# One unit of bit patterns in each of eight groups added up on VectorE, in an attention and MLP block on one Trainium2 core

## The chip, the core and the metric

The kernel runs on one core of one Trainium2 chip. The metric is device time in microseconds (us) of one execution; lower is better. A matmul instruction runs on TensorE (PE in the profile; PEld is its weight load), the exponentials of the softmax on ScalarE (ACT), evictions and bit arithmetic on VectorE (DVE) and GpSimd (POOL), and SyncE (SP) issues the transfers.

## The reference

```python
xn = _layernorm(x)                                  # x: 1 x 2048 x 640, bf16
q, k, v = (xn @ wqkv) split into 32 heads of 20
p = softmax(q @ k.T * 20**-0.5)                     # per head, 2048 x 2048
s = (p @ v, heads joined) @ wo
h = gelu(layernorm(xn) @ w1), its four quarters shifted by 1, -1, 2, -2 rows
x1 = xn + h @ w2
g = silu(x1 + gelu(layernorm(x1) @ w3) @ w4)
out = x + s * g
```

## The kernel before

**Groups.** The attention is worked off in 32 groups: eight quads of four heads, times four chunks `qc` of 512 queries. For each group 16 tiles of 128 keys are scored. A score tile of one head is one matmul with 32 rows of contraction in one of four row groups of the array ("row mode", the matmul of L1623); where a tile stands alone in the order it is done as four products over 32 columns each ("column mode", L1640). The method `score_pair` issues both. A switch between row mode and the column mode of all other products costs time, so the order gathers score tiles into bursts.

**Two ways to an exponential.** Most score tiles go to ScalarE, which writes exp of 1024 scores at a time (L1692, 730 times, plus 13 of double width at L1669). The others go to VectorE: `score_both` turns a score into a number whose 16 bits, read as bf16, approximate the exponential (L1714, 512 scores at a time, into the buffer `U`). One such pattern is coarse, so `block_bits` averages four: pattern 0 is `U` itself, patterns 1, 2 and 3 are `U` plus 32, 64 and 96 in the integer domain, each in one of three buffers `SS`. Patterns 1 and 2 of the unit touched here are made by VectorE (L1602, 4096 numbers), pattern 3 by GpSimd (L1600). A unit holds two blocks; a block is one pair of key tiles.

**Products.** The weights of pattern 0 and pattern 1 are the values `VA` unscaled (`EXP_W` is 1.0 for both), those of patterns 2 and 3 are a scaled copy `VP`. For each block and each pattern there is one product task, four matmuls over the four heads that run side by side (L1614), all accumulating in one PSUM bank. So a unit has eight product tasks. Exponentials of ScalarE are multiplied at L1432.

**Other work in the same stream.** TensorE also does all projections and both MLP branches in column mode (L733, 4 matmuls side by side), whose results VectorE evicts. At the end the output projection (`wob` tasks, L733) is multiplied by the gate on VectorE (L1845), and `cmb` adds the input tile, on GpSimd for the first twelve of 16 row tiles (L1911). Its input tile is fetched by SyncE (L1835) into one of two slots `XR`. The first product of a `wob` tile waits until the `cmb` two tiles earlier has read its slot.

**Order.** Which instruction follows which on each engine is written out in one long string, `TABLE`: two characters name a task, and one more each PSUM or SBUF slot that it takes. `follow` reads it, and `plan_sync` sets the semaphores from the tasks' reads and writes. The engines then run freely; each takes its instructions strictly in that order. The durations given to `T(...)` are a planner's costs; on the chip they do nothing. `lock=True` marks work of VectorE and GpSimd that is kept apart: a GpSimd task also waits for the last such VectorE task ahead of it in the string. `AGAIN` names score tiles that are issued once or twice more, into the same bank with the same result; before the change six products are repeated in this way. `ACC` is a dictionary from group to blocks whose patterns 0 and 1 are summed; it is empty before the change.

Of the kernel before, what the change touches and what calls it, by code (L numbers as in the profile page):

```python
# [656 lines left out]
class Gen:  # L657
# [1229 lines left out]
    def finish_qc(self, qc):  # L1887
# [8 lines left out]
        for nl in range(4):  # L1896
# [14 lines left out]
            T("pool" if onp else "dve", 1420 if onp else c_dve(cfg.D, "2x"), lambda e, sl=sl, addend=addend, res=res: e.tensor_tensor(res, SB2[:, sl, :], addend, op=ALU.add),  # L1911
# [234 lines left out]
    r"F+<%+=&'O''P'Q'R'S+.'+/(&E*v'G+9#+#'Z']$+>&'T+:$+X&+0'+W%+;$+8'^'_+Z+,'++('`'a*x+_#+K%+[+`$+J&+-#+?'b+c&F$+H(#7+G'+1*u+V$+b+L)+U%+o&&G&O&*w,+)*y+I$(P+n'+r'''"
    r"H*|,*(+Y#*t*{,,(&P+M+q,.&+u$,-%+x,/&+v#+y+|*z+A'+^(+])*~*},K$+@&,J%+a)'f&'g,#+B$'h'i'j+h('l$+F'k,L'+i''m'n+N,:&+j%+f$&0,;%,>+e#'o+d,=+s(+t''p'q+g$,0,A%,D,9#,"
    r"8$,B&,E+k+w)'r$+m(,<&+l'+p(+O-.'s't,@%,G$,H#,I$,?&&i'u'v'w+P'x#'y,C%'z'{'|'},N$,O#,W(,Z,X),P#+~,M(Q,w&,x%&p,&,),`',R$,_(,[,Q#,F'c#8'[3%+Q05(M$,c,y',b(N,p&,s%"
    r",S)'~,q'+z+{,t$->)-?(,',r&,u(-@$+},T,e,(,~&-2#-#%-1$(#,5',$-5-4,v,%,i-$#,4((%$(&(',]&,6&,1#,2$,^%,f((()(+#(,,3),a((-(.,{#(*-8(,z$-;,7,g-&%-%&(O(R-9),k-<,|%,d"
    r"-H(-K,U#,V$-'&,l,}(/(0-G)-J,Y)-0&-/%-3%-(($,h-M(-L'-N#-O$-R,j,o,n-P#-k%-j&(1$-Q-U(2-6'-l)-E$-7(-F#.`(Y(a-:((3(4-I',m-)(7((5(8(6-A(-B'(9-=-p&-C&-g#.%)-s-h$(:("  # L2150
    r";-_.$((<-i%-X-*.&#-D(Z#-x&-c$(=-w%+R-[-d#-{-z-e$([(](^-u)06-v((_(`-y&-m.1&-q%-~#-}$-W-V-t.((.2'.)).#)-Z(S(.4.*%-a$.5-`#(T(U.+'.8(.;-b'.9).,&.'(V.<(v(W(X.?-n$"
    r"-o#.-(-f-]/8'-r)/9&./(.0).3'(>../:((w((x(y.7#.6$.:%-Y&1(z-T({-^.I&.>+S.B-S.M#.L$(|.J#(@-|&b.H(?(.N)(A(B.A.D.d(.S'.E.T&.U'.c).=.K.g.P%.O$.Q$0I&.f0J.j(.m.V'.k)"
    r".W&0K.X%.n0L0M.h%.i$.l&.b(.@0N.y&.|/k'/n.a).R.Y.G.q#(E.p$.z%.}.F-+/$&.e#(C(D.s(/%'/(.r).t).C.u'/'.Z07(08.~#/#$09.w'/E(/F)/H/&%/I.x&0:0;.{$0<)(-,(}(F/*.o/5#/6"
    r"$/?(.v/@'.[/4/7#0=$0>0?/U&/+/V%/<$/=#0@/A)0A0C#/.0B/>&/W$450D0E0F0G0H/{)/J#/|(--/K$/;/B/1(~()#/N%)$/D'0P0O/C&/S$/R#)%/,/}#/T(/G')&/-/0)'/L(/M)/Y#/Z$/O/)///X/"
    r"P0#&/j(/~'/^%/Q/d)/m/[)0$$/]$(b&(c/g/c(/b&/a'(d(e0Q(f/_%/f/i$/h%0*)0)(/`(g/e'/q0%/l(/30+)/t)//20R#0S0&$0T/z4O(4R0U/w0V0X$0'$(o0Y0Z0[48(0-&0W4E#4F$0,%4G#0.&49"
    r"'/o/v.]0(0]4;/r4<4H#0^4I$4J'4@(4C/s4N'4?)4>%4=&0/4Q/x/p4U#&Z4S'4T(.^4V$/u/y4B4A$4W(4M&4X4Y004]4L%0_$0`0a014P&46$47#4j'4:)4k(0b0c0d4l%4K0e(0f0g4q$4r#5#&0h0i4s"
    r"#5&0j4w'4z5))5((5*'4D4f4x&4v#4u$4y$(p((q4~'5,(5+)(r4{(s(t57#Ef56$50&4^4Z5%5-)5/'51)4`52((u5559%5:(53&4_5.5J#5I$4a4[4c58&4}')=4|(5<545;4b5K'5$)5H5s5T)5?4o$4n#"
    r"4p&)>()?5S(4h'4g&5')@4d)A5B)B4e5L#5U(5b(5a)5M$(h)C4t5>4i)))(5d5X&5W'5e)*._4m5N$5Z$5^5Q()K5[#5P)5Y#)+5R)),5`'5_&5])-5=5v)5c%5u$5w(5E).5z025t#5V5@5x&6L%5y5~'6K"
    r"&5A5m5}(6%6M(6+#6*$6$5O5G5|)6'&6(%5C6,%6))5D5F61'5{(5g6I$6H#6J$5i5h5f60&(i((j(k5j5k5l6/#6.$64636#'5n6_&)D0k6^'68)67((l6&6;6:0l(m6-62#65#6O)66$6N7H6P(6=(n6b')"
    r"E#)R)F)G6>6m&69)6S#6Q&6R$6T$6n%)H)I6G0m$0n0o)J6@6o%03046X(6A0p6Y'6g#6f$6<6U6]6?6W%6V&6[6D6i))L#)M6h(6j(6Z$6`#6k#6c6a$6d)N)O)P6{%)Q6|&6e6B6v#6t)6w$6u(6y6z6l)0"  # L2160
    r"#7#&6x$7<%7=&)1)26~)6q#7%7>'6}(7$6p$)3)47:&79%716r()o7;#)56C76)72$7+73#75(5o77)6F6s6E7()7()8)97?7.)674(7@&):);)<0q)Y)S&)T)h)U)V7P$8~7A#5p7Q%)W)X7T'787L(7I&7K"
    r")7J'7,7B7)7h#7M)7O7N7g$7k(8(%7R(8)&8*&7S'7&7'7-7U7V7b(7c)7`#0s7a$70)a7f7d#7/7e7*7C8>%8?&8@%)Z#8,)7j#7i$)v7m5q8-(7l)[)]7W7v8&%80$8%&:V8/#8'))^)_8;(82)`8.$8<)7"
    r"n7y8='84%86#8183&87#)b#8+8E)898F(85$8A888G))c8K#8d&8e%)d8N)e)f8g(8f&8h)8:8L$)g8O8B%7p8i'8C&)i#)j)k0r8n(8D#8k#8o)8p%8l$)l)m7s)p(8H8m$)q)r)n8S&)}8V8R'8v(8u)8w)"
    r"8j7r8J$8I#8U)s)t)u8r(8Q'8M(8P&0t8s)8q7x7q8Y8T&7o)w&8X7z%7[&7]'8t#7D7^$7{$7|%)x)y)z){)~%En$*#*$*%*&)|7w*'Eo9&&9)9-$9B#5r7E9E9%%Ep8[7u7tEqErEz%909(*(E{E|Eh#EiE"
    r"j*)EkEl8Z9,%EsEm9/9<)9C$3#Et&EuE}Ev9?E~Ew11)123H$3IEx34#3;(3<3=3>3?8]9F3@13F#8c3J3K3L3M35361437387X$7Y%9;(150u$0v0wEy0x8x0y3&&3'3(3)8`399>163*0z3+1%#1&9I1'1("
    r"1)1*9@)7Z&9A(8_8^7~$92%93&9D(7}#8W8a7_3B$3C3D3E3F8#)95'9$$F%96(9##8b94$8$3G8y3-(3.3/0{)0|0}9'&309L97%9T$9S#9*)0~1#31329U)9+(1=#9.#1$1>1?1@9899$9O9:#9e&1A9J?C"
    r"9r(9d%9q)9h911B9g9=%9K9u&9s'9t'9l#9o9k$9G9M17(9V(9n9W):W18199v$9X&1:1;9b&9c':%#:&$9w9R1<:(:)9Z)9[(:^9H1U(:-#:09f#9{&9]%9|'9P1V1W9}(:,$:*):+(1X:.$1Y9Y1C&9^&:/"
    r"1Z9_'9`):_:31D1E9Q9y$9j(9i)9x%1F1G1H9N9m'9a1+#:o8z1,1-:a1.1/109z):#(:$)1b&1c1d:9:A%:@&?M$:>'1e:'&1f9p1I$:`7F:B%:=(9~1J1K1L:X:b?P1g:Z:c:[:K$1M1N:6:?#:L':1:G':"
# [112 lines left out]
```

## Time and profile before

| what | value |
|---|---|
| median of three runs | 781.76 us (780.97 to 783.34) |
| the profiled execution | 782.75 us, of which its span is 780.9 us |
| granted TensorE clock, mean | 0.999 |
| ScalarE busy | 763.0 us, 98% |
| TensorE matmul busy | 770.5 us, 99% |
| VectorE busy | 698.9 us, 89% |
| GpSimd busy | 441.4 us, 57% |

Times in the profile count from the first instruction. A line such as `L1602 DVE TENSOR_SCALAR out<-in x91 | 110.4, 1225 | 2.0 <-PE` is one group of instructions: source line, engine, operation, shapes, how many; their busy time in us, the mean of one in ns; the idle time of the engine just before them and what ended it. Records of neighbouring instructions on one engine overlap a little, so that the pitch from start to start is shorter than a record.

### The profile page before, as it was taken

What the parts mean: (1) busy time and instruction counts of PE and PEld (TensorE: products, weight loads), DVE (VectorE), ACT (ScalarE), POOL (GpSimd) and SP (SyncE); (2) the same over time, 40 slices, a digit from 0 to 9 for tenths busy, and PEclk for the clock granted to TensorE, in tenths of its full rate; (3) what the DMA queues carried; (4) which work ended last, traced back from release to release, by engine and by line L of the source; (5) the groups of instructions that cost most, each with busy time, mean ns of one, the idle gap of its engine ahead of it and who ended that gap; (6) DMA issues with size and microseconds to landing.
All of it is one profiled execution on the core that took longest, in us unless ns stands there. A gap on an engine that the chain in (4) does not pass through costs nothing.

```text
span 780.9 us, 27979 instructions
## 1 busy us (share of the span) xinstructions
PE 770.5 (99%) x12470; PEld 291.4 (37%) x12470; DVE 698.9 (89%) x1170; ACT 763.0 (98%) x803; POOL 441.4 (57%) x238
## 2 busy tenths in 40 slices
PE   8999999999999999999999999999999999999997
PEld 4433332334434333233434333333334333333454
DVE  8889899988999999988988889998989889897786
ACT  7999999999999999999999999999999999999986
POOL 5676646544566656466564664766454456645733
PEclk9999999999999999999999999999999999999999
DMA  5232532450122333432242331334421123014443
GB/s 174 41 109 59 128 90 58 120 121 24 29 45 54 76 81 76 102 64 45 54 92 55 82 71 33 67 69 69 122 55 29 30 45 87 16 23 136 116 125 104
DMA packets 141352, 58.12 MB, mean 74 GB/s; under 512 B 113728, under 2 KB 136432, under 8 KB 141232
## 3 DMA queue, kind: packets, MB, share of 16 engines
q1 hardware_dynamic: 141232, 56.33, 31.0%
q8 instruction: 98, 1.61, 0.8%
q14 instruction: 22, 0.18, 0.1%
HBM read 34.70 MB, written 10.33 MB: 58 GB/s over the span
## 4 chain that ended last, share of the span: by engine, by line
PE 57%; ACT 40%; DVE 1%; DMA 1%; issue 0%; POOL 0%; SPq 0%
ACT arena L1692 35%; PE psum L733 21%; PE psum L1623 16%; PE psum L1614 10%; PE psum L1432 7%; PE psum L1640 1%; ACT arena L2095 1%; ACT arena L1669 1%; ACT arena L2003 1%; DMA arena<-in_A_x_dram 1%; ACT arena L2123 1%; PE psum L1489 1%; PE psum L1463 1%; PE psum L1493 0%; ACT L1692 0%; PE psum L1079 0%
## 5 line engine op out<-in xcount | busy, mean ns | idle before, releaser
L1692 ACT ACTIVATE arena<-psum 128x1024 bf16<-128x1024 f32 x730 | 676.7, 1106 | 6.6 <-PE psum L1623 4.0
L1600 POOL TENSOR_TENSOR arena<-arena 128x2048 int32<-128x2048 int32 x92 | 330.2, 3598 | 195.9 <-DVE arena L1602 106.3
L1714 DVE TENSOR_SCALAR arena<-psum 128x512 uint16<-128x512 f32 x528 | 341.6, 682 | 36.2 <-PE psum L1623 28.4
L733 PE MATMUL psum<-arena 128*32 128x320 bf16 (+1 forms) x5808 | 331.6, 333 | 0.8 <-POOL arena L1911 0.7
L1623 PE MATMUL psum<-arena 32*128 32x512 bf16 x1908 | 254.3, 384 | 1.6 <-ACT arena L1692 0.6
L1614 PE MATMUL psum<-arena 128*22 128x512 bf16 x2112 | 183.5, 382 | 0.0
L733 PEld LDWEIGHTS psum<-arena 128*32 128x32 bf16 x5808 | 135.6, 96 | 121.1 <-issue 48.6
L1623 PEld LDWEIGHTS psum<-arena 32*128 32x128 bf16 x1908 | 68.2, 91 | 223.4 <-ACT arena L1692 113.3
L1432 PE MATMUL psum<-arena 128*22 128x512 bf16 x1456 | 137.9, 382 | 0.0
L1602 DVE TENSOR_SCALAR arena<-arena 128x4096 uint16<-128x4096 uint16 (+1 forms) x121 | 130.3, 1091 | 2.6 <-PE psum L1614 1.2
L1614 PEld LDWEIGHTS psum<-arena 128*22 128x22 bf16 x2112 | 46.5, 90 | 64.2 <-issue 46.0
L1746 POOL TENSOR_TENSOR arena<-arena 128x512 bf16<-128x512 f32 x30 | 41.7, 1390 | 46.5 <-DVE arena L1602 35.6
L1432 PEld LDWEIGHTS psum<-arena 128*22 128x22 bf16 x1456 | 34.9, 90 | 44.7 <-issue 33.4
L2088 DVE CAST arena<-psum 128x512 bf16<-128x512 f32 x48 | 32.6, 681 | 2.8 <-PE psum L733 2.8
L1299 DVE CAST arena<-psum 128x512 bf16<-128x512 f32 x40 | 27.1, 682 | 6.2 <-PE psum L733 6.0
L1640 PE MATMUL psum<-arena 128*32 128x512 bf16 x328 | 32.1, 381 | 0.0
L1911 POOL TENSOR_TENSOR arena<-arena 128x640 bf16<-128x640 bf16 x12 | 16.8, 1399 | 22.5 <-DVE arena L1539 9.2
L944 DVE BATCH_NORM_STATS2 arena<-arena 128x6 f32<-128x320 bf16 x54 | 24.3, 476 | 2.0 <-DMA arena<-in_A_x_dram 2.0
L1669 ACT ACTIVATE arena<-psum 128x2048 bf16<-128x2048 f32 x13 | 25.6, 1969 | 0.1
L1845 DVE SCALAR_TENSOR_TENSOR arena<-psum,arena 128x320 bf16<-128x320 f32 x32 | 15.2, 482 | 9.1 <-PE psum L733 9.0
L1733 DVE STREAM_TRANSPOSE arena<-psum 128x512 f32<-128x512 f32 x30 | 21.3, 710 | 2.1 <-PE psum L1623 0.9
L2117 DVE TENSOR_TENSOR arena<-psum,arena 128x320 bf16<-128x320 f32 x32 | 15.6, 486 | 6.8 <-PE psum L733 6.6
(135 smaller groups left out, 339.6 us busy)
## 6 DMA issues: line engine op xcount, KB each, us to landing
arena<-in_B_w_dram SPq DMA_DIRECT2D x48, 160.0 KB, 2.7
arena<-arena SPq DMA_DIRECT2D x124, 32.0 KB, 1.9
arena<-in_B_w_dram SPq DMA_DIRECT2D x4, 960.0 KB, 5.5
arena<-in_A_x_dram SPq DMA_DIRECT2D x8, 320.0 KB, 6.0
arena<-in_A_x_dram SPq DMA_DIRECT2D x16, 160.0 KB, 2.4
out_dram<-arena SPq DMA_DIRECT2D x16, 160.0 KB, 2.2
heads<-arena SPq DMA_DIRECT2D x120, 20.0 KB, 2.0
arena<-queries SPq DMA_DIRECT2D x28, 80.0 KB
```

What stands on the lines that cost most here:

```text
L733: ins = e.matmul(pb[32 * c:32 * c + 32, 0:N], lhsT(k, c), rhs(k, c), start=(k == 0), stop=(stop and k == nk - 1), tile_position=(0, 32 * c))
L1432: ins = e.matmul(pb[32 * i:32 * i + 22, 0:512], VA[:, ql, kts[i // 2], i, :], PT[:, slots[i // 2][0].slot, slots[i // 2][0].at(i % 2):slot ...
L1600: return e.tensor_tensor(dst.bitcast(I32), U[:, ub, 0:w].bitcast(I32), bass.AP(c.tensor, c.offset, [list(c.ap[0]), [0, w // 2]]), op=ALU.add)
L1602: fa if onp else lambda e, v=v, dst=dst: e.tensor_scalar(dst, U[:, ub, 0:w], EXP_B[v], None, op0=ALU.add),
L1614: ins = e.matmul(pb[32 * i:32 * i + 22, 0:512], wv, dst[:, at:at + 512].bitcast(BF16), start=first, stop=final, tile_position=(0, 32 * i))
L1623: return e.matmul(out, self.KT[32 * i:32 * i + 32, b, 128 * kt:128 * kt + 128], q, start=True, stop=True, tile_position=(32 * i, 0))
L1640: ins = e.matmul(out[32 * c:32 * c + 32, :], self.KT[:, b, 128 * kt + 32 * c:128 * kt + 32 * c + 32], self.QM[:, gb, i, :], start=True, st ...
L1669: lambda e: e.activation(self.PT[:, hp[0].slot:hp[0].slot + 2, :], self.psum[:, 512 * h0.slot:512 * h0.slot + 2048].rearrange("p (a b) -> ...
L1692: lambda e: e.activation(self.PT[:, hp.slot, :].rearrange("p (a b) -> p a b", b=512), self.banks(hs), AF.Exp, scale=cfg.scale),
L1714: T("dve", c_dve(512), lambda e, h=h, y=y: e.tensor_scalar(U[:, ub, y:y + 512], self.bank(h.slot)[:, :], a_exp, EXP_BIAS, op0=ALU.mult, op ...
L1746: return e.tensor_tensor(OnT.rearrange("p (k d a) -> p a k d", k=4, a=4), Ob[:, :].rearrange("p (a k d) -> p a k d", a=4, k=4), in1, op=AL ...
L2088: T("dve", c_dve(512), lambda e, h=h, fc=fc, i=i, G=G: e.tensor_copy(G[:, i, fc, :], self.wbank(h)[:, 0:512]), reads=[wa], writes=at, name ...
```

## The change

For eight groups (one in each quad) the unit with blocks 2 and 3 gets two new VectorE instructions, each 2048 numbers wide: they add `U` (pattern 0) to the buffer of pattern 1, both read as bf16, in place. The product tasks of pattern 0 of that unit are gone; the products of pattern 1 now take the sum. That is 16 adds more and 16 product tasks (64 matmuls of L1614) fewer in the whole kernel. The code for such a sum was there before, as a transfer issued by GpSimd, but with `ACC` empty it never ran. `AGAIN` becomes empty, so the six repeated score products go. The planner's cost of `cmb` on GpSimd goes from 1420 to 2000. And the string with the order is another one from its 385th entry of 6,939 on, which lies in the first group of the first quad; from there the two orders differ in detail. No other instruction is added or removed.

```diff
--- before.py
+++ after.py
@@ -582,7 +582,7 @@
         self.W7 = (0, 1)
         self.LAST = [[[4, 2]], [[3, 2]]]
         self.HP = True
-        self.AGAIN = {(3, 1, 10, 2): 1, (7, 1, 2, 1): 1, (7, 1, 6, 2): 1, (7, 1, 12, 1): 2, (7, 1, 15, 0): 1}
+        self.AGAIN = {}
         self.EARLY = 4
         self.ND = ([2, 4, 4, 4],) + tuple([5, 4, 5, 4] for _ in range(5)) + ([5, 5, 5, 5], [5, 5, 4, 4])
         self.PP |= {(quad, qc, 0, 2) for quad in range(8) for qc in range(4)}
@@ -594,6 +594,7 @@
         self.NR[6][1] = (107,)
         self.NR[6][3] = ()
         self.NR[7][1] = (107,)
+        self.ACC = {(0, 1): (2, 3), (1, 1): (2, 3), (2, 1): (2, 3), (3, 0): (2, 3), (4, 1): (2, 3), (5, 0): (2, 3), (6, 2): (2, 3), (7, 0): (2, 3)}
         self.ND = ([2, 4, 4, 4], [5, 4, 4, 4], [5, 4, 4, 4], [5, 4, 4, 4], [5, 4, 5, 4], [5, 4, 5, 4], [5, 4, 5, 4], [5, 4, 4, 4])
 
 
@@ -1601,9 +1602,10 @@
                 T("pool" if onp else "dve", 90 + 0.925 * w if onp else c_dve(w, "4x"),
                   fa if onp else lambda e, v=v, dst=dst: e.tensor_scalar(dst, U[:, ub, 0:w], EXP_B[v], None, op0=ALU.add),
                   reads=halves + ([A("CI", v)] if onp else []), writes=dsta, name=f"s{quad}_{qc}_{blocks[0][0]}_{v}", lock=True, due=self.at(self.nact, f"s{quad}"))
-            if acc and v == 1:
-                T("pool", 1000, lambda e, dst=dst: e.dma_start(dst.bitcast(BF16), U[:, ub, 0:w].bitcast(BF16), accum_op=ALU.add, max_dma_last_dim=4096),
-                  reads=halves + dsta, writes=dsta, is_dma=True, nbytes=2 * 256 * w, name=f"acc{quad}_{qc}_{blocks[0][0]}", stream="acc", lock=True)
+            for x in range(len(blocks) if acc and v == 1 else 0):
+                y = slice(2048 * x, 2048 * x + 2048)
+                T("dve", c_dve(2048, "2x"), lambda e, dst=dst, y=y: e.tensor_tensor(dst[:, y].bitcast(BF16), dst[:, y].bitcast(BF16), U[:, ub, y].bitcast(BF16), op=ALU.add),
+                  reads=halves + dsta, writes=dsta, name=f"acc{quad}_{qc}_{blocks[0][0]}" + "y" * x, lock=True, due=self.at(self.nact, f"s{quad}"))
             for n, (j, kts, units) in enumerate([] if acc and v == 0 else blocks):
                 def fn(e, v=v, dst=dst, n=n, j=j, kts=kts, units=units):
                     pb = self.bank(self.PVB)
@@ -1908,7 +1910,7 @@
                     self.wo_mult("wob", n, hh, range(cfg.KC + (qc not in cfg.W7)), SB2[:, sl, :], A("SB2", sl, hh))
             res, resa = (addend, adda) if split else (OS[:, sl, :], [A("OS", sl)])
             onp = n in cfg.PC
-            T("pool" if onp else "dve", 1420 if onp else c_dve(cfg.D, "2x"), lambda e, sl=sl, addend=addend, res=res: e.tensor_tensor(res, SB2[:, sl, :], addend, op=ALU.add),
+            T("pool" if onp else "dve", 2000 if onp else c_dve(cfg.D, "2x"), lambda e, sl=sl, addend=addend, res=res: e.tensor_tensor(res, SB2[:, sl, :], addend, op=ALU.add),
               reads=adda + [A("SB2", sl, 0), A("SB2", sl, 1)], writes=resa, name=f"cmb{n}", lock=True, cls=-2 if split and nl > 1 else 0)
             T("sp", C_SP, lambda e, res=res, n=n: e.dma_start(outv[:, n, :], res),
               reads=resa, writes=[("out", n)], is_dma=True, nbytes=128 * cfg.D * 2, name=f"st_out{n}", stream=f"out{sl}" if n < self.cfg.NT - 1 else "out2",
@@ -2141,109 +2143,109 @@
...
-    r"&2)&J&K(G(J&L*7*0&,'@&3&%*_&*`%*a$*J$*K#*H(&M*I)*L'*M&?#&@&A*N(L#4'A3$&B&C&4(&D*Q&+'$(K&5+(#*E*P(*T*O)&=(*F'/)&N+)&&>'0'1*S#&q#*W#*X$'2'3*Y(&r&s*R%*[(*Z)&t&u"
...
+    r"&2)&J&K(G(J&L*7*0&,'@&3&%*_&*`%*a$*J$*K#*H(&M*I)''*M&?#&@*L'&A&B&C*N&4(&D&5+'#*Q&+($*P(*O)+)#'/#'0*E*T&=('1'2&q)*F*X#*S&*W$&>#4'3&r*Y)&s*Z('4*[)*R%&t*U*V&u+3"
...
```

More of the change, by code (lines that the diff above doesn't have):

```diff
@@ L2147 @@
[L2147 to L2166, printed above, removed]
@@ new lines @@
+    r"$&v+2#*c%*]%*h'*b&+4'*i('I$'J'K'L'M+$#+%$(L*k*d&*l+&('.'N(K*^*G*p'&/&i*n(*s*m)*q)*o&'5('6'7'8'9*r+5$'A+T':&E+6#&N+7%+**e'U$*g&+D'+C(*v*f%*j#'V'W'X'B''Y'C'D'E"
+    r"'Z'F+E('O&+=%+<&+>$'P*y'Q'R&p'S'G'T'H3$*|+.)+/(+0&+#+:$+X%+[+W&+9#+8']#'^'_++(+;)+,)+Z'`'a'b+_%+b+K#+J$+`&+c+?*t&F#+-%+G(+L'+H)&G+1+I)&O(+U$+o&+V#+Y#*w&P*u+n"
+    r"'+r,*(+q,+)*{*x+v%,,$+y+u&,.$,-#*z,/%+M'f#+^)+]('g+x+|'h+@#+A$,K%+a),J&'i'['j*~'e+B&+h(,L'+i)'k(Q*}+F+j&'l&'m'n,;$,:%+e'+f&'o'p+N,>+g('q,=,0+t(+s)+w$+d,8$,9#"
+    r"+l',B&,<#,E+k,A%+m('r$'s't'u,G#,D+O+P,H$+p),?%,@&,I%'v'w,C&'x#'y'z'{'|,O$,N#'},X(,W),[,P(,Z,),w&,x%,F,_',`(#7,#,c,y)3%,&,Q#,R$+}+z,q)-.'~,b,S&,t%'c,p(,r#,',M"
@@ new lines @@
+    r"&Z,s$,u%+~(#+{,~#-?'-2&-5->((M$-#$-@'+Q(N,T,$(O,%,1',z(,2&,(05,v-$&,4%,5$,3$(%&(&,6((',^',]&,a#(((),d,{)(Y(+((,,|%,i,e,7,V&,U'(-,k(*,f-%#-9(-&$-<,Y$-8)(.(/-'"
+    r"(,h,o-0&-/'-;-H(,j-(-M#-L$(0-G),}#8-K-J-3#-1%-4-P&-O(-j&-k',g-N)-R(7&(8(9-l%-F%-6',l-E&-7(-:)(:,m-Q($(1$(2,n(3-I$-A'-B(-U-h$(4(5-g%-)-_-C((6-=-i$(;-X(<-*-p&."
+    r"`(P.%'.$((Z$([-d$-c#-x%-W(=-[-s.&)-D-u'-{-w&-v(-e&(](^(_&0-z-}#(`.2%-~$-V-y(-Y-m-q'.5.((.)).1&.#'-T-`$-a%-t.4.*$.'(S&(T.8(.9).+'.;-b%.,&(R+R(v06+S(E(U(V-n$-o"
+    r"%.<-f(W.-#.0&./'-r)(X/8(/9)-S-Z/:'(@.?.=.6$.7#.3&-|.>(w(-](x.B.:%(y.I&.J((z({..-^(>(?&(A.L$(|.M%.H.D(B.d'.T).c&&b.S(.P#.g.N#.K.U%.@.O$0I(0J.k'.f.W(.V).n.Q$.j"
```

176 lines of the change are left out of this document (94 added, 82 removed).

## The prediction

> **What bounds the kernel now.** I read the page first, then the busy times by stretch, then the groups by shape, and last the waits and the places where ScalarE stands.
>
> ```profile
> span 780.9 us, 27979 instructions
> PE 770.5 (99%) x12470; PEld 291.4 (37%) x12470; DVE 698.9 (89%) x1170; ACT 763.0 (98%) x803; POOL 441.4 (57%) x238
> PE 57%; ACT 40%; DVE 1%; DMA 1%; issue 0%; POOL 0%; SPq 0%
> ```
>
> Busy times by stretch (PE, PEld, DVE, ACT, POOL, then clock, DMA share, GB/s):
>
> ```profile
> 20.00:100.00 80.00, 79.93 (x1255) 28.39 (x1247) 71.35 (x127) 78.81 (x90) 50.94 (x39) 1.00 0.35 85
> 100.00:200.00 100.00, 99.92 (x1515) 35.12 (x1517) 90.77 (x137) 99.30 (x98) 54.07 (x20) 1.00 0.34 82
> 200.00:300.00 100.00, 99.88 (x1592) 36.81 (x1595) 96.06 (x173) 99.23 (x107) 57.33 (x28) 1.00 0.25 53
> 300.00:400.00 100.00, 99.72 (x1486) 35.26 (x1482) 91.30 (x150) 99.45 (x98) 59.56 (x32) 1.00 0.31 67
> 400.00:500.00 100.00, 99.96 (x1629) 37.94 (x1627) 89.10 (x144) 99.90 (x107) 57.99 (x25) 1.00 0.32 69
> 500.00:600.00 100.00, 99.94 (x1540) 35.67 (x1540) 92.55 (x137) 99.34 (x98) 57.00 (x21) 1.00 0.35 73
> 600.00:700.00 100.00, 99.19 (x1501) 34.70 (x1497) 88.84 (x134) 100.00 (x108) 49.92 (x18) 1.00 0.19 39
> 700.00:760.00 60.00, 58.94 (x1139) 27.44 (x1131) 49.09 (x77) 57.94 (x62) 35.68 (x18) 1.00 0.44 121
> ```
>
> From 20 to 760 us ScalarE is busy for 734.0 of 740 us: it stands 6.0 us in all, 2.1 of them after 700. The change takes no work from ScalarE, so nearly the whole gain that any change on another engine can bring lies in those 6 us, in what the records hide (below), and in the stretch after 760.
>
> ```profile
> L1692 ACT ACTIVATE arena<-psum 128x1024 bf16<-128x1024 f32 x730 | 676.7, 1106 | 6.6 <-PE psum L1623 4.0 <-PE psum L1489 2.0
> 604.53 24.75 ACT arena L1692 x27
> ```
>
> 730 exponentials take 676.7 us, 0.927 each, while the 27 from 604.53 us take 24.75, 0.917 each including the last one's end. So short waits of up to 730 x 0.010 = 7 us hide inside busy time. All of ScalarE's idle time here ends with TensorE: the exponential waits for its scores.
>
> **TensorE is close behind.** Its 99% are ends that the profile models. I price its work by pitches instead.
>
> ```profile
> 307.23 1.91 PE L733 MATMUL psum<-arena 128*32 128x512 bf16 x32
> 304.62 0.39 PE L1432 MATMUL psum<-arena 128*22 128x512 bf16 x4
> 304.94 0.41 PE L1623 MATMUL psum<-arena 32*128 32x512 bf16 x4
> 305.28 0.83 PE L1614 MATMUL psum<-arena 128*22 128x512 bf16 x12
> 760.96 1.80 PE L733 MATMUL psum<-arena 128*32 128x320 bf16 x48
> L1623 PE MATMUL psum<-arena 32*128 32x512 bf16 x1908 | 254.3, 384 | 1.6 <-ACT arena L1692 0.6 <-DVE arena L1714 0.2
> L1614 PE MATMUL psum<-arena 128*22 128x512 bf16 x2112 | 183.5, 382 | 0.0
> L733 PE MATMUL psum<-arena 128*32 128x512 bf16 x2320 | 170.9, 381 | 0.1
> L733 PE MATMUL psum<-arena 128*32 128x320 bf16 x3488 | 165.7, 300 | 0.7 <-POOL arena L1911 0.7
> L1432 PE MATMUL psum<-arena 128*22 128x512 bf16 x1456 | 137.9, 382 | 0.0
> L1640 PE MATMUL psum<-arena 128*32 128x512 bf16 x328 | 32.1, 381 | 0.0
> ```
>
> Eight tasks of four 512-wide products take 1.91 us with one record's end of 0.39: (1.91 - 0.39) / 7 = 0.217 us per task. Twelve of 320: (1.80 - 0.30) / 11 = 0.136. A burst of row-mode scores costs, from the column task before it to the one behind, 305.28 - 304.62 - 0.217 = 0.44 us. The written order has 581 bursts. Sum: 6,216 / 4 x 0.217 = 337 (2112 + 2320 + 1456 + 328 products of 512), 872 x 0.136 = 119, 581 x 0.44 = 256, and some 20 for the small groups: 732 of 781 us. So TensorE has some 6% of reserve, ScalarE 2%, VectorE 11%.
>
> **The change part by part.**
>
> *Products removed.* 16 tasks of L1614: 16 x 0.217 = -3.5 us of TensorE work.
>
> *Repeats removed.* Six scores of L1623, inside bursts: -6 x 0.217 at most, -1.3 us.
>
> *The new order.* I read the string of the change entry by entry with the same numbering of tasks. Applied to the string of before this gives 82 score tiles in column mode, which are the 328 products of L1640, and 1908 row products, as the rows above have it. The string of the change has 103 tiles in column mode (+21 x 0.217 = +4.6 us), 1881 row products (27 fewer, of them the six repeats) and 575 bursts. Six bursts fewer are -2.6 us at 0.44, if the remaining ones are no longer than before; when 21 tiles and six bursts only trade places with column tasks it is nearer 0. TensorE in all: -3.5 - 1.3 + 4.6 - 2.6 = -2.8, and with the bursts at zero and the repeats hidden beside other row groups +1.1. I take -1 us of work. So most of what the products leave is given back by how the scores are issued. On a path that TensorE sets 57% of, -1 us is worth -0.6; in the ScalarE-bound stretches it is worth nothing. I take -0.3, between -1.6 (57% of 2.8) and +0.6.
>
> *Adds on VectorE.* The trace has no bf16 add of 2048.
>
> ```profile
> 317.29 2.36 DVE L1602 TENSOR_SCALAR arena<-arena 128x4096 uint16<-128x4096 uint16 x2
> L1602 DVE TENSOR_SCALAR arena<-arena 128x4096 uint16<-128x4096 uint16 x91 | 110.4, 1225 | 2.0 <-PE psum L1614 0.9
> L1253 DVE TENSOR_REDUCE arena<-arena 128x1 f32<-128x2048 bf16 x5 | 11.4, 2274 | 0.0
> L1868 DVE SCALAR_TENSOR_TENSOR arena<-psum,arena 128x640 bf16<-128x640 f32 x3 | 2.5, 821 | 0.7 <-PE psum L1857 0.7
> L1884 DVE TENSOR_TENSOR arena<-arena 128x640 bf16<-128x640 bf16 x4 | 1.9, 484 | 0.0
> L1602 DVE TENSOR_SCALAR arena<-arena x121: 649/1216/1772, 43.2 to 748.8; 128x4096 uint16<-128x4096 uint16 x91, 128x2048 uint16<-128x2048 uint16 x30
> ```
>
> The in-place bf16 add of 640 (L1884) takes 0.484 us, the pass over 640 that reads PSUM 0.821: per element the add goes at about twice the other's rate. At the slow rate 2048 take 2.27 us (L1253). At twice it they take about half, which is the record of a pattern of 4096 (1.22), whose pair at 317.29 has a pitch of 2.36 - 1.22 = 1.13 us. I take 1.13, since L1884 is the same operation: 16 x 1.13 = +18.1 us of VectorE work; by L1253 it would be 36. VectorE is idle for 781 - 699 = 82 us, so in sum it fits. The cover is thin in places: 200 to 300 us is 96% full, and two adds there are 2.3 us of the 3.9 left.
>
> *What waits for an add.* Pattern 0's products could run as soon as `U` was written; now TensorE, which works strictly in order, needs the second add first. In the string of before, 2, 3, 4, 4, 2, 9, 5 and 2 exponentials lie between the start of pattern 1 and its first product, in the eight units in turn; in the new one, 2, 1, 2, 2, 1, 4, 0 and 3 between the start of the second add and its product. The reserve falls from 31 x 0.92 = 29 us to 15 x 0.92 = 14 us for eight units, of which the adds' own 1.13 us each use 9.
>
> ```profile
> PEld psum L1623 <- ACT arena L1692: 113.3, 304, 0.7
> PEld psum L1623 <- DVE arena L1714: 34.2, 92, 0.5
>   DVE arena L1602: 0.8, 3
> ```
>
> So far products hardly wait for patterns: the last row is what L1614 waited for L1602, 0.8 us over 121 patterns. Scores wait for a bank that VectorE frees (L1714) in 92 places, and every add put ahead of an eviction can lengthen such a wait. If an add passes a tenth of its length on to TensorE, it costs 16 x 0.11 = +1.8; bounds are 0 and, with every add passed on in half, +9. Judged by the 0.8, I take +0.8.
>
> [...]
>
> *The planner's cost of `cmb`.* It does nothing on the chip, but it moves the end of the order.
>
> ```profile
> arena<-in_A_x_dram SPq DMA_DIRECT2D x2, 160.0 KB, 3.2
> 754.56 1.39 POOL L1911 TENSOR_TENSOR arena<-arena 128x640 bf16<-128x640 bf16 x1 [2.10 <-DVE arena L1740]
> 756.01 0.39 PEld L733 LDWEIGHTS psum<-arena 128*32 128x32 bf16 x16 [1.00 <-POOL arena L1911]
> 757.10 5.61 ACT L1692 ACTIVATE arena<-psum 128x1024 bf16<-128x1024 f32 x6 [1.28 <-PE psum L1489]
> ```
>
> Here a `cmb` starts late, most likely because its input tile landed late (two loads of 3.2 us in the mean between 749.9 and 753), TensorE stands 1.0 us for it, and ScalarE 1.28 us behind that, its longest stand after the start. In the old string the load of that tile is issued two exponentials ahead of the product that stood; in the new one, four (+1.8 us). This stand should go: between -1.28 and 0, I take -1.0. The same stretch has no slack on TensorE to give it away again, but a later load can land late too.
>
> **Sum**, from the profiled execution's own 782.75 us: ScalarE 0, TensorE -0.3, adds +0.8, `cmb` -1.0: -0.5. The median is 781.76, so 781.3 there. A difference of under 0.3% (2.3 us) is what a measurement of this kernel can't tell from no change.
>
> **Rivals.**
>
> *Faster: TensorE's work is worth its full price.* For it: every stand of ScalarE ends with TensorE, and 57% of the chain is TensorE's. Against: the count of the order, above. If the whole 4.8 us of products and repeats counted along that chain, 0.57 x 4.8 = -2.7, with the `cmb` at -1.28 it is -4.0: 777.8.
>
> *Slower: the adds come between VectorE's evictions and TensorE's next scores.* Place: units (1,1), (4,1) and (6,2), where the order leaves 1, 1 and 0 exponentials, and 200 to 300 us, where VectorE is 96% full. It decides when VectorE reaches the second add more than about 0.9 us late. Price: half of every add on the path, +9, less the `cmb`: 781.8 + 9 - 1 = 789.8; at a quarter, 785.3. Against it stands the 0.8 us. [...]
>
> [...]
>
> [...]
>
> [...]
>
> **How the numbers follow.** No change within 0.3% (781.3): 0.40. Faster rival: 0.32. First slower rival: 0.24, the second 0.04. So faster 0.32, same 0.40, slower 0.28. The range takes in the faster rival with a little more, and the first slower one to near its upper price: 776.5 to 788.5. The likeliest case alone runs from 779.4 to 784.1.
>
> **What would show it.** The adds as 16 records of 1.2 us on VectorE (2.3 would make the sum wrong); L1614 at 2048 products, L1640 at 412, L1623 at 1881; ScalarE's busy time unchanged at 763 and its stand at 757 gone; VectorE at some 716 us. TensorE waiting for the adds by more than 2 us in all, or for L1714 by more than 36, would show the slower rival; ScalarE's stands between 100 and 700 us falling well below 2.8 us, the faster one. An end of the last exponential that moves by more than 2.3 us either way makes the prediction wrong.

## The result and the profile after

The changed kernel takes 789.33 us (median of 4 runs, 788.67 to 789.60) against 781.86 us of the kernel before beside it (780.97 to 783.34): ratio 1.0089, 95% interval 1.0076 to 1.0101. It is slower by 0.9%, 0.8 us above the range of the prediction. The profiled execution took 789.6 us, of which its span is 787.5. In the source of after, lines from 595 to 1604 are numbered one higher than before and those behind 1605 two higher: the exponential L1692 is now L1694, the eviction L1714 is L1716, the scores L1623 are L1625, the products L1614 are L1616; the adds are L1607.

The page of after, its span, its engines and its chain by engine:

```profile
span 787.5 us, 27952 instructions
PE 776.7 (99%) x12451; PEld 296.1 (38%) x12451; DVE 715.4 (91%) x1186; ACT 765.7 (97%) x803; POOL 440.4 (56%) x238
PE 65%; ACT 31%; DVE 2%; DMA 1%; POOL 0%; SPq 0%; issue 0%; DVEq 0%
```

Busy times of after by the same stretches (PE, PEld, DVE, ACT, POOL, then clock, DMA share, GB/s):

```profile
20.00:100.00 80.00, 79.83 (x1238) 28.28 (x1226) 71.95 (x124) 78.20 (x89) 50.86 (x40) 1.00 0.34 80
100.00:200.00 100.00, 100.00 (x1514) 36.23 (x1515) 94.08 (x141) 98.61 (x98) 50.15 (x18) 1.00 0.36 85
200.00:300.00 100.00, 99.91 (x1594) 37.73 (x1582) 95.94 (x173) 98.90 (x107) 61.06 (x29) 1.00 0.26 54
300.00:400.00 100.00, 99.53 (x1471) 35.37 (x1463) 93.63 (x151) 98.81 (x98) 58.66 (x33) 1.00 0.32 69
400.00:500.00 100.00, 99.99 (x1605) 37.98 (x1597) 91.19 (x146) 99.19 (x107) 55.74 (x23) 1.00 0.33 66
500.00:600.00 100.00, 99.97 (x1482) 34.44 (x1482) 92.85 (x141) 99.32 (x99) 57.53 (x22) 1.00 0.34 73
600.00:700.00 100.00, 99.29 (x1527) 36.43 (x1527) 91.17 (x133) 99.20 (x105) 51.82 (x18) 1.00 0.16 38
700.00:760.00 60.00, 58.82 (x1071) 26.10 (x1075) 48.91 (x76) 58.28 (x60) 33.33 (x17) 1.00 0.44 105
sum 740.00, PE 737.34 PEld 272.56 DVE 679.73 ACT 730.52 POOL 419.16; mean PE 92.17 PEld 34.07 DVE 84.97 ACT 91.31 POOL 52.39
```

ScalarE stands for 740 - 730.5 = 9.5 us of this stretch, before it was 6.0. Its busy time rose by 2.7 us with the same work, so most likely the short waits inside the records grew too. 3.5 + 2.7 = 6.2 of the 6.6 us of span are found on ScalarE.

The groups of after by shape:

```profile
L1694 ACT ACTIVATE arena<-psum 128x1024 bf16<-128x1024 f32 x730 | 678.2, 1087 | 9.7 <-PE psum L1625 5.9 <-PE psum L1490 2.4
L1625 PE MATMUL psum<-arena 32*128 32x512 bf16 x1881 | 259.0, 384 | 2.2 <-ACT arena L1694 1.1 <-DVE arena L1716 0.3 <-ACT arena L1671 0.2
L1616 PE MATMUL psum<-arena 128*22 128x512 bf16 x2048 | 178.4, 381 | 0.0
L1642 PE MATMUL psum<-arena 128*32 128x512 bf16 x412 | 40.1, 380 | 0.2
L1607 DVE TENSOR_TENSOR arena<-arena 128x2048 bf16<-128x2048 bf16 x16 | 19.5, 1216 | 0.1
```

And of its waits (who waited for whom: us in total, times, longest):

```profile
PEld psum L1625 <- ACT arena L1694: 106.9, 288, 0.7
PEld psum L1625 <- DVE arena L1716: 31.8, 91, 0.6
POOL arena L1601 <- DVE arena L1607: 23.9, 4, 7.6
POOL arena L1748 <- DVE arena L1607: 12.8, 2, 7.0
POOL arena L896 <- DVE arena L1607: 8.2, 1, 8.2
PEld psum L1616 <- DVE arena L1603: 3.0, 10, 0.4
```

The work is what the prediction counted: 2048 products, 1881 and 412 scores, 16 adds of 1.22 us. The description of the change says that no other instruction is added or removed; that holds for the tasks, but 21 score tiles that were one row product each are four column products in the new order (412 against 328), which is why the row products fell by 27 and not by the six repeats alone. Nobody but GpSimd waited for an add, and the scores waited no longer for evictions than before (34.2 us then). By these rows the adds are not what the time was lost to, and the question of the experiments is what was.

I numbered ScalarE's 786 instructions in both traces and took the start of each after minus before. The lag grows in small steps: +0.9 us by 90 instructions, +1.7 by 180, +2.6 by 270, +3.1 by 360, +4.4 by 510, +4.7 by 540 to 675, +5.8 by 690, +7.2 by 765, +6.6 at the end. It rises at thirteen places by 0.3 to 0.9 us and at others by less, and falls back at a few; no single place makes it.

### The profile page after: what moved, and what is told of

The parts are those of the page before. It is cut to its first block, busy times and chain, and to the rows that moved or that the text cites. A ratio compares the mean times of both kernels' runs of the same rounds, so it can differ in the third digit from the quotient of the medians.

```text
span 787.5 us, 27952 instructions
## 1 busy us (share of the span) xinstructions
PE 776.7 (99%) x12451; PEld 296.1 (38%) x12451; DVE 715.4 (91%) x1186; ACT 765.7 (97%) x803; POOL 440.4 (56%) x238
## 4 chain that ended last, share of the span: by engine, by line
PE 65%; ACT 31%; DVE 2%; DMA 1%; POOL 0%; SPq 0%; issue 0%; DVEq 0%
ACT arena L1694 27%; PE psum L734 25%; PE psum L1625 18%; PE psum L1616 11%; PE psum L1433 8%; PE psum L1642 2%; ACT arena L2097 1%; ACT arena L1671 1%; DMA arena<-in_A_x_dram 1%; ACT arena L2125 1%; DVE arena L1716 1%; PE psum L1490 1%; DMA arena<-heads 0%; POOL arena L1601 0%; PE psum L1464 0%; PE psum L1494 0%
## 5 line engine op out<-in xcount | busy, mean ns | idle before, releaser
L1694 ACT ACTIVATE arena<-psum 128x1024 bf16<-128x1024 f32 x730 | 678.2, 1087 | 9.7 <-PE psum L1625 5.9
L1716 DVE TENSOR_SCALAR arena<-psum 128x512 uint16<-128x512 f32 x528 | 341.1, 682 | 33.0 <-PE psum L1625 24.1
L734 PE MATMUL psum<-arena 128*32 128x320 bf16 (+1 forms) x5808 | 335.5, 333 | 0.1
L1625 PE MATMUL psum<-arena 32*128 32x512 bf16 x1881 | 259.0, 384 | 2.2 <-ACT arena L1694 1.1
L734 PEld LDWEIGHTS psum<-arena 128*32 128x32 bf16 x5808 | 136.2, 96 | 124.3 <-issue 51.8
L1616 PE MATMUL psum<-arena 128*22 128x512 bf16 x2048 | 178.4, 381 | 0.0
L1625 PEld LDWEIGHTS psum<-arena 32*128 32x128 bf16 x1881 | 70.2, 91 | 220.3 <-ACT arena L1694 106.9
L1433 PE MATMUL psum<-arena 128*22 128x512 bf16 x1456 | 139.0, 382 | 0.2 <-ACT arena L1694 0.2
L1616 PEld LDWEIGHTS psum<-arena 128*22 128x22 bf16 x2048 | 45.1, 90 | 61.2 <-issue 42.6
L1642 PE MATMUL psum<-arena 128*32 128x512 bf16 x412 | 40.1, 380 | 0.2
L2097 ACT ACTIVATE arena<-arena 128x6144 bf16<-128x6144 bf16 x4 | 21.1, 5316 | 0.0
```

What stands on the lines that cost most here:

```text
L734: ins = e.matmul(pb[32 * c:32 * c + 32, 0:N], lhsT(k, c), rhs(k, c), start=(k == 0), stop=(stop and k == nk - 1), tile_position=(0, 32 * c))
L1433: ins = e.matmul(pb[32 * i:32 * i + 22, 0:512], VA[:, ql, kts[i // 2], i, :], PT[:, slots[i // 2][0].slot, slots[i // 2][0].at(i % 2):slot ...
L1616: ins = e.matmul(pb[32 * i:32 * i + 22, 0:512], wv, dst[:, at:at + 512].bitcast(BF16), start=first, stop=final, tile_position=(0, 32 * i))
L1625: return e.matmul(out, self.KT[32 * i:32 * i + 32, b, 128 * kt:128 * kt + 128], q, start=True, stop=True, tile_position=(32 * i, 0))
L1642: ins = e.matmul(out[32 * c:32 * c + 32, :], self.KT[:, b, 128 * kt + 32 * c:128 * kt + 32 * c + 32], self.QM[:, gb, i, :], start=True, st ...
L1694: lambda e: e.activation(self.PT[:, hp.slot, :].rearrange("p (a b) -> p a b", b=512), self.banks(hs), AF.Exp, scale=cfg.scale),
```

## The experiments

Times are medians; each ratio is to the kernel before, run beside it on the same chip. "Old" and "new order" are the strings of before and after.

**The adds or the order.** Theory A: the adds hold up VectorE and so the scores. Theory O: the order itself is slower. First the new order with adds of 16 numbers, which leaves most of the sum out:

```diff
-                y = slice(2048 * x, 2048 * x + 2048)
+                y = slice(2048 * x, 2048 * x + 16)
```

> The new order as it is, but each of the 16 adds takes 16 numbers in place of 2048, so that the sum is left out (nearly all of pattern 0 of the eight units is missing from the result). Before 781.9 us, after 789.3. Theory A (the adds hold VectorE for 16 x 1.13 us, bank evictions come late, TensorE stands): the 6.4 us of added stands go, 782 to 784. Theory O (the new order itself puts column products ahead of scores, the adds matter little): 787 or more.

789.13 us, 1.0093 (1.0079 to 1.0107). In the new order the 19.5 us of adds cost 789.33 - 789.13 = 0.2 us, which is less than the spread of either kernel's runs. Theory A falls there.

Then the sum in the old order: the entries of the 16 products gone from the string, each unit's two adds put right behind the making of pattern 1, and the repeats kept.

```diff
-        self.AGAIN = {}
+        self.AGAIN = {(3, 1, 10, 2): 1, (7, 1, 2, 1): 1, (7, 1, 6, 2): 1, (7, 1, 12, 1): 2, (7, 1, 15, 0): 1}
```

> The order of before, and in it only the change itself: in the eight units the two adds stand right behind the making of pattern 1, the 16 products of pattern 0 are taken out, the six repeats stay. Theory A: 787 or more, as slow as the new order. Theory O: 780 to 783.5. If both have a share, 784 to 786.

803.08 us, 1.0270 (1.0256 to 1.0284). The same with adds of 16 numbers:

> The kernel above with adds of 16 numbers in place of 2048 (the sum is left out): what 16 products fewer are worth without the adds. If TensorE's work counts along the chain of waits, 0.57 x 3.5 = 2.0 us faster than before, 779.9; if at full price 778.4; if ScalarE is the wall, nothing, 781.5 to 782.

782.66 us, 1.0009 (1.0000 to 1.0018). So in the old order the 16 removed products are worth nothing, and the adds cost 803.08 - 782.66 = 20.4 us. The timeline of the old order with the sum shows one unit (start, us, engine, line, what it waited for):

```profile
325.90 1.23 DVE L1603 TENSOR_SCALAR arena<-arena 128x4096 uint16<-128x4096 uint16 x1
327.16 2.48 DVE L1607 TENSOR_TENSOR arena<-arena 128x2048 bf16<-128x2048 bf16 x2
...
329.56 1.22 DVE L1603 TENSOR_SCALAR arena<-arena 128x4096 uint16<-128x4096 uint16 x1
330.70 0.68 DVE L2090 CAST arena<-psum 128x512 bf16<-128x512 f32 x1
...
331.44 0.09 PEld L1625 LDWEIGHTS psum<-arena 32*128 32x128 bf16 x1 [2.37 <-DVE arena L2090]
...
333.46 1.02 ACT L1694 ACTIVATE arena<-psum 128x1024 bf16<-128x1024 f32 x1 [2.80 <-PE psum L1625]
```

VectorE makes two patterns and two adds in 4.9 us without freeing a bank in between. The eviction at 330.70 comes late, the score behind it stands 2.37 us and ScalarE 2.80. This is the slower rival of the prediction, at more than its full price, but in an order that isn't the changed kernel's.

The fourth run has the new order with the old work, the 16 products back in place of the adds:

> The new order with the work of before: no adds, and the 16 products of pattern 0 stand where the adds stood. Nothing is left out. Theory O: as slow as after or slower by the products, 788 to 792. Theory A: as before and up to 2 us more, 782 to 784.

792.29 us, 1.0132 (1.0118 to 1.0146): with the same tasks but for the repeats, and 23 score tiles more in column mode (420 products of L1640 against 328), the new order is 10 us slower than the old. Without products and adds the two stand 789.13 to 782.66: theory O, 6.5 us.

**What the repeats are worth.** Only `AGAIN` emptied, in the kernel before:

```diff
-        self.AGAIN = {(3, 1, 10, 2): 1, (7, 1, 2, 1): 1, (7, 1, 6, 2): 1, (7, 1, 12, 1): 2, (7, 1, 15, 0): 1}
+        self.AGAIN = {}
```

> The kernel before with the six repeated score products gone and nothing else. The prediction has them inside bursts, beside other row groups, and at most 1.3 us of TensorE work: 781.0 to 782.1 beside 782.1 of before. If the repeats kept something in step (a bank, the clock), it would be slower than before by more than 1 us.

782.39 us, 0.9999 (0.9991 to 1.0008): nothing.

**How much room for VectorE each order has.** Half adds in the old order, and slow ones in the new:

```diff
-                y = slice(2048 * x, 2048 * x + 2048)
+                y = slice(2048 * x, 2048 * x + 1024)
```

> The order before the change with the sum, where full adds cost 20.4 us against adds of 16 numbers (803.1 against 782.7); here each add is 1024 numbers wide, half of the sum is left out, and by the record of 2048 (1.22 us) one takes some 0.65. If every microsecond of VectorE in those places is passed on: 9.6 to 11 us, 792 to 794. If the order holds a reserve of some 0.5 us for each unit and passes on what is above it: 786 or less. If already a short one loses a whole place for an eviction: 798 or more.

789.19 us, 1.0089 (1.0076 to 1.0103). Its group of adds:

```profile
L1607 DVE TENSOR_TENSOR arena<-arena 128x1024 bf16<-128x1024 bf16 x16 | 11.1, 692 | 0.5
```

789.19 - 782.66 = 6.5 us for 11.1 us of adds, between the first theory and the second. The other half costs 13.9 us.

```diff
-                T("dve", c_dve(2048, "2x"), lambda e, dst=dst, y=y: e.tensor_tensor(dst[:, y].bitcast(BF16), dst[:, y].bitcast(BF16), U[:, ub, y].bitcast(BF16), op=ALU.add),
+                T("dve", c_dve(2048, "2x"), lambda e, dst=dst, y=y: e.tensor_tensor(dst[:, y].bitcast(BF16).rearrange("p (a b) -> p b a", b=2), dst[:, y].bitcast(BF16).rearrange("p (a b) -> p b a", b=2), U[:, ub, y].bitcast(BF16).rearrange("p (a b) -> p b a", b=2), op=ALU.add),
```

> The changed kernel with each add reading and writing its 2048 numbers in steps of two, the even ones first and then the odd ones: the same sums, by a slower pass, by the rates in the trace of before about 2.2 us instead of 1.2, so +16 us of VectorE work in the places of the adds. If the new order holds more room for VectorE than the adds use: under 791. If it holds just their length: each further us is passed on as in the old order, 789.3 + 16 x 1.0 to 1.1 = 805. Half of it: 797.

828.18 us, 1.0585 (1.0562 to 1.0607), above every theory. Its group of adds:

```profile
L1607 DVE TENSOR_TENSOR arena<-arena 128x2048 bf16<-128x2048 bf16 x16 | 41.7, 2607 | 0.1
```

VectorE has 41.7 - 19.5 = 22.2 us more to do, and the kernel takes 38.9 us more. So the new order holds room for adds of 1.2 us at 0.2 us in all, and not for adds of 2.6. What lies behind the 1.75 for each further microsecond is taken up in the last section.

**Whether an engine's load explains the new order.** Theory "place": it has no reserve on TensorE around the units. Theory "spread": it is tighter everywhere. In the new order without adds, products of patterns 2 and 3 were cut to one matmul of 16 columns, in the touched units and then in others:

```diff
+                    few = v > 1 and acc and not first and not final
-                    for i in range(4):
+                    for i in range(1 if few else 4):
+                        m = 16 if few else 512
```

> The order after the change, each add 16 numbers wide as in the second run of this study's kind, and in the eight touched units the products of patterns 2 and 3 cut to one matmul of 16 columns (unless one begins or ends the accumulation of its bank): part of the weighted sum is left out. That takes up to 32 x 0.2 = 6.4 us from TensorE in just the places where the adds stood. Theory 'place' (the new order has no reserve on TensorE around these units, and its 6.5 us over the old order are lost there): the time falls by most of it, to 783 to 785 us. Theory 'spread' (the new order is tighter everywhere, the units are no special place): it falls by the share that TensorE sets on the whole, 1 to 3 us, to 786 to 788, the same as with products cut elsewhere. If ScalarE or the banks set the time there: no change, 789.

789.44 us, 1.0094 (1.0080 to 1.0107), with 28 products cut.

> As the first of these runs, but the same number of products is cut in eight other groups, two groups away from the touched ones in the same quad (part of the weighted sum is left out). Theory 'place': little gain, 787.5 to 789. Theory 'spread': the same gain as there, 786 to 788.

788.82 us, 1.0084 (1.0071 to 1.0098), with 30 cut. The old order with 29 cut in the units:

> The same cut of the products of patterns 2 and 3 in the eight units, in the order before the change without products of pattern 0 and with adds of 16 numbers (part of the weighted sum is left out). Taking 16 products there was worth nothing (782.7 against 782.1), so both theories expect 781.5 to 782.7 here; under 780 would say that TensorE's work does set the time in the old order too, only with more products.

783.43 us, 1.0019 (1.0008 to 1.0029), a little above what was expected. Some 6 us of TensorE work (28 x 0.217) are worth nothing in either order, as sums. Both theories fall. So the 3.2 us that the fourth run lost to 16 products are no general price of TensorE's work; they hang, most likely, on the place where those stood, two more in a row with the two of pattern 1.

Then VectorE was unloaded:

```diff
-            T("dve", c_dve(512), lambda e, h=h, y=y: e.tensor_scalar(U[:, ub, y:y + 512], self.bank(h.slot)[:, :], a_exp, EXP_BIAS, op0=ALU.mult, op1=ALU.add),
+            m = 512 if self.unit < 4 else 256
+            T("dve", c_dve(512), lambda e, h=h, y=y, m=m: e.tensor_scalar(U[:, ub, y:y + m], self.bank(h.slot)[:, 0:m], a_exp, EXP_BIAS, op0=ALU.mult, op1=ALU.add),
```

> The order after the change with adds of 16 numbers; from the fifth unit on, each eviction of a score tile for VectorE's exponentials takes 256 of its 512 columns, so part of those weights is left out (stale). An eviction becomes some 0.25 us shorter and its bank comes free earlier. Theory 'banks' (in the new order ScalarE stands where a score waits for a bank that an eviction or the exponential right ahead of it frees, at 317, 494, 679, 744 and 750 us): the evictions' part goes, at least 2.5 us, to 786.5 or less. Theory 'columns' (ScalarE stands because the new order puts runs of column products ahead of its scores, whatever the banks do): no change, 788.5 to 789.3.

789.05 us, 1.0084 (1.0070 to 1.0098): the evictions' part of theory "banks" falls, and the time is the one that theory "columns" named, 788.5 to 789.3.

> The same short evictions in the order before the change, without the 16 products and with adds of 16 numbers (782.7 without them). In that order only one stand of more than 0.2 us, of 0.29, follows a bank that an eviction freed, so theory 'banks' expects 0.3 to 1 us, 781.7 to 782.4; theory 'columns' no change, 782.7.

782.02 us, 1.0002 (0.9992 to 1.0012). In the page VectorE's busy time fell from 715.4 us of the changed kernel to 586.7 in the first of the two, and ScalarE's stands did not move. The stands of ScalarE over 0.3 us from 60 to 740 us, in us, each in front of the same instruction of its sequence:

| at, in after | after | no adds | 28 products fewer | short evictions | before |
|---|---|---|---|---|---|
| 78.35 | 0.55 | 0.55 | 0.55 | 0.55 | 0 |
| 118.62 | 0.54 | 0.54 | 0.54 | 0.51 | 0.55 |
| 162.76 | 0.48 | 0.48 | 0.48 | 0.48 | 0 |
| 247.85 | 0.41 | 0.41 | 0.41 | 0.41 | 0.41 |
| 257.71 | 0.37 | 0.37 | 0.37 | 0.37 | 0 |
| 317.32 | 0.63 | 0.63 | 0.63 | 0.62 | 0 |
| 339.03 | 0.50 | 0.50 | 0.50 | 0.50 | 0.08 |
| 494.18 | 0.46 | 0.46 | 0.46 | 0.46 | 0 |
| 510.45 | 0.37 | 0.37 | 0.17 | 0.37 | 0 |
| 679.47 | 0.66 | 0.66 | 0.66 | 0.66 | 0 |

With 15 or 129 us less on VectorE or 6 less on TensorE they stay within 0.03, but for that at 510 us. (In the run with 30 products cut elsewhere that at 494 us moves too, from 0.46 to 0.34.) A stand that none of these loads moves is made by the order. In these traces two things in the order make one. The first is the choice of banks. The timeline of after around the first stand:

```profile
75.75 2.04 ACT L1694 ACTIVATE arena<-psum 128x1024 bf16<-128x1024 f32 x2
...
77.82 0.14 PEld L1625 LDWEIGHTS psum<-arena 32*128 32x128 bf16 x4 [0.42 <-DVE arena L1716]
77.83 0.43 PE L1625 MATMUL psum<-arena 32*128 32x512 bf16 x4
...
78.35 1.94 ACT L1694 ACTIVATE arena<-psum 128x1024 bf16<-128x1024 f32 x2 [0.55 <-PE psum L1625]
```

and in that of the run with short evictions:

```profile
73.41 4.13 ACT L1694 ACTIVATE arena<-psum 128x1024 bf16<-128x1024 f32 x4
...
77.57 0.43 PE L1625 MATMUL psum<-arena 32*128 32x512 bf16 x4
...
78.09 1.02 ACT L1694 ACTIVATE arena<-psum 128x1024 bf16<-128x1024 f32 x1 [0.55 <-PE psum L1625]
```

One exponential ends at 75.75 + 2.04 = 77.79, the scores start at 77.83, the next exponential at 78.35. By the string, one of its two score tiles lies in the bank that the exponential just ended had to free: ScalarE has no pair in reserve, and stands from its own end to the end of a score. I read from both strings, for each exponential, which one frees its scores' banks. It is the one right ahead 3 times in the old order and 7 times in the new; the new ones of these stand at 78, 163, 339, 756 and 770 us, and one of the old, at 744 us, is no longer among them.

The second is a run of column products written ahead of the scores. Around the stand at 257 us:

```profile
254.30 3.04 ACT L1694 ACTIVATE arena<-psum 128x1024 bf16<-128x1024 f32 x3
...
256.39 0.39 PE L1616 MATMUL psum<-arena 128*22 128x512 bf16 x4
256.61 0.71 PE L734 MATMUL psum<-arena 128*32 128x320 bf16 x16
257.26 0.60 PE L1625 MATMUL psum<-arena 32*128 32x512 bf16 x5
257.71 1.02 ACT L1694 ACTIVATE arena<-psum 128x1024 bf16<-128x1024 f32 x1 [0.37 <-PE psum L1625]
```

The banks of these scores were freed at 256.43, by the string and the trace, when the exponential two ahead ended. TensorE comes to the scores 0.83 us later, behind column products that follow each other without a pause from 255.27 on. At 510 us it is the same (banks free at 509.17, scores at 509.96). At 317, 494 and 679 us evictions free the banks; with short evictions they do so 0.55 to 1.8 us before the scores start, and the stands stay within 0.01. Where a run with fewer products happened to shorten such a run of column products by one task, the stand behind it shrank: at 510 us from 0.37 to 0.17, at 494 us from 0.46 to 0.34. So these five are theory "columns", shown by a trial at two places and read from the traces at the other three. In all, the cut products gave no time back: in the run with 28 cut, a stand at 750 us grew from 0.79 to 1.27. And at 78 us both causes end together: the run of column products also reaches the scores at 77.83, so that stand alone doesn't show a price of banks.

**Whether the choice of banks alone has such a price.** The kernel before, every engine's sequence as it was, with the PSUM banks of 14 pairs of neighbouring exponentials' score tiles exchanged. In the string only the third character of the four entries of each such pair differs, here for quad 1, chunk 3, key tiles 0 and 2:

```diff
-95'
-9$$
-96(
-9##
+95#
+9$(
+96$
+9#'
```

> The kernel before, with every engine's sequence as it was; only the PSUM banks of 14 pairs of neighbouring score tiles for ScalarE are exchanged, spread from 104 to 641 us, so that 12 exponentials more than before (15 instead of 3) have scores in a bank that the exponential right ahead of them must free. Theory 'banks by order': each such place makes ScalarE stand for the time from the end of one exponential to the end of a score, 0.55 us (the stand of that kind at 117.64 us of before), with some loss behind it: 12 x 0.55 = 6.6 us or more, 788 to 793. If TensorE's work or VectorE's set the time there, whatever the banks: under 784.

791.51 us, 1.0122 (1.0108 to 1.0135): +9.5 us, 0.8 for each of the 12 new places. There ScalarE stands for 0.48 to 0.73 us each, 6.4 in all. The trace of before around one of them, and then that of this run:

```profile
193.75 7.43 ACT L1692 ACTIVATE arena<-psum 128x1024 bf16<-128x1024 f32 x8
...
197.72 0.39 PE L1623 MATMUL psum<-arena 32*128 32x512 bf16 x3
```

```profile
197.75 1.07 ACT L1692 ACTIVATE arena<-psum 128x1024 bf16<-128x1024 f32 x1
...
198.87 0.39 PE L1623 MATMUL psum<-arena 32*128 32x512 bf16 x3 [0.70 <-ACT arena L1692]
...
199.32 1.94 ACT L1692 ACTIVATE arena<-psum 128x1024 bf16<-128x1024 f32 x2 [0.51 <-PE psum L1623]
```

Before, eight exponentials run on end while the scores go ahead. Here the scores wait until the exponential has ended (197.75 + 1.07 = 198.82), and ScalarE stands 0.51 us. The theory of banks by order holds: same work, same sequences, and a loss larger than the whole change's. It shows what such a choice can cost where TensorE would otherwise be ahead; it doesn't show that the new order's loss is of this kind.

**Where in the new order the price lies.** At two points, near 130 and 500 us, both orders have done the same tasks, so there they can be joined:

```diff
-        self.ACC = {(0, 1): (2, 3), (1, 1): (2, 3), (2, 1): (2, 3), (3, 0): (2, 3), (4, 1): (2, 3), (5, 0): (2, 3), (6, 2): (2, 3), (7, 0): (2, 3)}
+        self.ACC = {(0, 1): (2, 3)}
```

> The new order up to some 130 us (one of the eight units, with its two adds), the old order behind it with its products and repeats. Theory 'each stretch': the lag that the changed kernel has there, +0.9, stays: 783.0. Theory 'one place': 782, or most of the 7 us.

783.50 us, 1.0017 (1.0008 to 1.0025).

> The old order up to 130 us and from some 500 us on, the new one between, with four of the eight units. Theory 'each stretch': the lag gained there by the changed kernel, 3.7 - 0.9 = +2.8: 784.9. Theory 'one place': 782, or most of the 7 us.

785.71 us, 1.0050 (1.0037 to 1.0062).

> The old order up to some 500 us, the new one behind it, with three of the eight units and the end of the kernel, where the stand at 757 us is gone. Theory 'each stretch': 6.6 - 3.7 = +2.9: 785.0. Theory 'one place': 781 to 782, or most of the 7 us.

786.41 us, 1.0058 (1.0044 to 1.0071). One, four and three units cost +1.5, +3.7 and +4.4 us by the medians (783.50, 785.71 and 786.41 less 781.98 of the kernel before beside them). 1.4 of the last are made at the join: ScalarE's lag there goes from -0.31 to +1.13 between instructions 510 and 525, in the whole change from +4.35 to +4.39. Less that they add up to 8.2 or 8.3, near the 7.5 of the whole. The price goes with every stretch that holds touched units, and no part of the new order beats the old. No version tried beats the kernel before.

## Why the prediction was wrong, point by point

*The step that failed* is the paragraph "The new order". It read the new string as an amount of TensorE work ("I take -1 us of work", "-0.3") and gave no price to where the order puts the scores. With the products and the adds out of both, the new order costs 789.13 - 782.66 = 6.5 us. The prediction took it as neutral. It had the string, and counted from it the exponentials between an add and its product, which decided nothing. What bears on the stands is when the scores of the next exponential can start: which step frees their banks, and how many column products stand ahead of them. The stands at 257, 317, 494, 510 and 679 us, 2.5 us in all, come from runs of column products. Those of exponentials whose bank the one right ahead frees (3 before, 7 after) are partly of the other kind: at 339 us the scores wait for the bank, at 163 us one of two does, and at 78 and 756 us TensorE reaches the scores just as the bank comes free. How the 6.5 us divide between the two stays open, the more as 2.4 us lie inside ScalarE's busy time (765.7 us in the new order with adds of 16 numbers, 763.3 in the old), where no stand shows. That the order makes them, and not the loads, is shown.

*TensorE's work* was right as an amount and as a price: products 0, repeats 0, more cut products 0 in the time as a whole. That "nearly the whole gain that any change on another engine can bring lies in those 6 us" held too, and it is most likely why nothing came back.

*The adds* were sized rightly (16 x 1.22 us; "I take +0.8", measured +0.2). But the +0.2 holds only in an order that has their room built in. In the old order the same adds cost 20.4 us, more than twice the upper bound of 9. The prediction took the cover from VectorE's idle sum of 82 us; what counts is how long VectorE may stay away from the banks at that place.

*The `cmb` term* was taken from one execution. (Nor was its stand ScalarE's longest after the start: the last instruction of ScalarE waits 2.8 us in both kernels.) The stand at 757 us is 0.29 us in the changed kernel, as forecast, but there is one of 0.52 seven instructions ahead of it that the old order has not. And in ten profiles with the old end of the order that stand was 0.50 to 0.54 us six times and 0.97 to 1.28 four times, that of before among the four (the ten kernels differ elsewhere). So 1.28 was no fixed price, and the execution that showed it lay 1.0 us above its median. The new end saves 1.28 - 0.29 - 0.52 = 0.47 us against that profile, and against the six nothing.

*The faster rival* fell with the products' price of 0. *The second slower rival*, 0.04 of the forecast: no run shows its term, an add held up by a GpSimd pass, and none has an add without the lock. In the changed kernel the 16 adds took 1.202 to 1.225 us each, no GpSimd pass ran beside one, and GpSimd waited 23.9 + 12.8 + 8.2 us for them. The nearest thing in the trace of before is one pattern of L1602: it starts at 520.63, beside a pass of L1600 that ends at 517.72 + 3.60 = 521.32, and takes 1.77 us against a median of 1.22. *The first slower rival* named the right resource, the banks between VectorE and the scores, with the price of the old order, and looked for it in waits for the adds. Its signs stayed away in the changed kernel (no wait of TensorE for an add, 31.8 us for evictions against its 36), because the order's price lay elsewhere: in scores that start too late for ScalarE, behind column products or behind a bank that ScalarE itself has to free.

## What to carry to other kernels

When a change comes with a new written order, price the order as a part of its own: run it with the new work taken out and the old order with the old work taken out, and compare these two. Before counting work, read for each step of the engine that sets the time who must free the buffer of its next input, and how much other work stands ahead of the making of that input; a buffer freed by the step right ahead was here a stand of 0.48 to 0.73 us at each new place of the run with other banks, and of 0.50 us at 339 us of the new order, in all four runs of the table. And a stand seen in one profile is a term of the sum only if other executions have it too.
